# Two units' last keys and reciprocals turned together in a fused attention kernel

## The chip, the cores and the metric

The kernel runs on one core of one Trainium2 chip. The metric is the device time of one execution in microseconds (us). Engines are called as the profile calls them: PE is the matrix engine (TensorE) and PEld its weight loads, DVE the vector engine, ACT the scalar engine, POOL the general one (GpSimd), and SP the engine whose queue issues most transfers.

## The reference

Three layers follow each other on a batch of 4 sequences of 576 positions. The first is attention with 8 heads of 64 dimensions; queries and keys are rotated by position. The second is a gated two-layer product on the attention's output `x`, mixed with `x` shifted by one position. The third is a gated block with a product over positions.

```
scores = rotate(q) @ rotate(k).T / 8
attn = exp(scores - max(scores)); attn = attn / (sum(attn) + 1e-9)
x = attn @ v                                  # heads side by side: 512 columns
k = relu(mix(mu_k, x, x_prev) @ w_k) ** 2     # 512 -> 1024
x2 = sigmoid(mix(mu_r, x, x_prev) @ w_r) * (k @ w_v)
u, w = split(relu(x2 @ w_in)); w = (w - mean(w)) / sqrt(var(w) + 1e-6)
out = (u * (w_spatial @ w + b_spatial)) @ w_out
```

The change lies in the attention: where the exponentials and the reciprocal of their sum are turned (transposed) so that they can be multiplied with `v`.

## The kernel before

**Units.** Attention is cut into 72 units, 9 for each group of two head pairs, 18 for each sequence. A normal unit takes 128 query rows of one pair of heads, against all 576 keys of both heads. The fifth unit of each nine, the tail (`tail` in the code; units 4, 13, 22, ...), takes the last 64 rows of two pairs. Two normal units that follow each other share one tile `pt`, with the columns of the first at 0 to 127 and of the second at 128 to 255; `part` is 0 for the first and 1 for the second. The tail's columns stand at 256 to 319.

**The steps of a unit** (function `unit`). On PE: `scores` (L315 to L339) fills two PSUM tiles `s`, one for each head. On DVE: `top` (L342) takes the negated maximum of each head. On ACT: `expo` (L347) writes the exponentials to `p` (named `pf` in the profile) and their sums. Then `total` (L351, ACT), `norm` (L354, the reciprocal, DVE) and `spread` (L358, ACT, which writes the reciprocals 64 times side by side to `r`, named `rb`).

**Turning** is done by `turn(n)` on PE into one of two PSUM banks named `t`, and by `take(n)`, which copies the bank to `pt` and gives it free. For n = 0 and n = 1 it turns four blocks of 128 keys of head n (L378), and ACT copies 512 columns. The blocks start at key 0 for head 0 and at key 64 for head 1, so 64 keys of each are left over; they lie side by side in `p`. For n = 2 a normal unit turns these 128 keys (L380) and the spread reciprocals (L381), and DVE copies 256 columns to rows 8 and 9 of `pt`.

**Then** `values` (L402, named `v`) multiplies `pt` with `v` in 10 matrix instructions (the profile counts 20), of which the last two (four) read row 8; `gather` (L414, DVE) multiplies by row 9, the reciprocals. `values` runs after the second unit of a pair, or after the tail where the tail's columns belong to the pair too.

**The feed.** When the 18 units of a sequence are done, the second layer's first products for it (`feed`: `mk`, L498, and `mv`, L537, dots of 12 matrix instructions each) are given to PE among the units of the next sequence. The last sequence's feed has no attention beside it. Its first dot needs four chunks of mixed input, and the fourth is made from the last `gather` through a multiply (L466, ACT), an add (L470, DVE), a rounding (L476, ACT) and a difference (L479, DVE). While that feed runs, the weights of the later layers and the mixed input of the gate are loaded (`mix_steps`, L612, and the loads of L652); they wait until attention is closed.

**What sets the order.** All of this is written as steps with an engine, an estimated duration, the steps that it depends on and a rank. `Plan.order` (L62) plays the steps through: for each engine it takes, among the steps that could start soonest (on DVE and ACT within 0.3 us of that), the one of lowest rank, and it counts the room in PSUM: two `t` banks, two banks for `v` and the dots. The instructions of each engine are emitted in that order, and each engine works through its own in order. A scores step depends on both `expo` steps of the unit before, since there is only one pair of `s` tiles for each unit in flight; `expo` depends on the turns of the unit three before, whose `p` it overwrites.

After attention the remaining products (gate rows, mixing over positions, the projection) run from code written out in order (L692 to L844).

Of the kernel before, what the change touches and what calls it, by code (L numbers as in the profile page):

```python
# [7 lines left out]
F32 = mybir.dt.float32  # L8
# [8 lines left out]
B, H, S, D = 4, 8, 576, 64  # L17
# [9 lines left out]
WB, GB, WB2, GB2 = 3, 2, 3, 2  # L27
RAW, ROT, VB, PFB, PTB, XTS = 2, 4, 2, 3, 2, 6
KB, RLB, VSB = 4, 2, 1
EARLY, EVERY = 24, 2.9  # L30
# [74 lines left out]
def body(ctx: ExitStack, tc, qp, kp, vp, cs, mu_k, mu_r, w_k, w_v, w_r, w_in, w_sp, b_sp, w_out, out):  # L105
# [196 lines left out]

    units, scored, duos, freed = {}, {}, {}, {}

    def unit(m):
# [50 lines left out]
        def spread():  # L356
            st["r"] = at.tile([128, 2, D], F32, tag="rb", bufs=2, name=f"rb{m}")
            nc.scalar.copy(st["r"], st["sm"][:, 3, :].unsqueeze(2).to_broadcast([128, 2, D]))  # L358

        def turn(n, slot):  # L360
# [14 lines left out]
            elif n < 2:  # L375
                for c in range(4):
                    k = 64 * n + 128 * c
                    nc.tensor.transpose(pt[:, c, :], p[:, n, k:k + 128], ident)  # L378
            else:
                nc.tensor.transpose(pt[:, 0, :], p.rearrange("p a b -> p (a b)")[:, 512:640], ident)  # L380
                nc.tensor.transpose(pt[:, 1, :], st["r"].rearrange("p a b -> p (a b)"), ident)  # L381

        def take(n, eng):
            for u, d in enumerate(into):
                if "pt" not in d:
                    d["pt"] = at.tile([128, 10, 320], F32, tag=f"pt{d['n'] % PTB}", name=f"pt{d['n']}")
                o = d["pt"][:, 4 * n:min(4 * n + 4, 10), 256:320]
                if not tail:
                    o, x = d["pt"][:, 4 * n:min(4 * n + 4, 10), 128 * part:128 * part + 128], st["t", n]
                    x = x if n < 2 else x[:, 0:2, :]  # L390
                elif n < 2:
# [37 lines left out]
        nm = add("DVE", 0.17, norm, [t], m - 0.3)  # L429
        sp = add("ACT", 0.26, spread, [nm], m - 0.3)  # L430
        ready = [[exps[m, 0], exps[m, 1]] if tail else [exps[m, 0]], [exps[m, 1]], [sp]]
        for n in range(3):
            turned[m, n] = add("PE", (0.5, 0.5, 0.8)[n] if tail else (0.44, 0.44, 0.22)[n], lambda slot, n=n: turn(n, slot),
                               ready[n], m + 0.1 * n, take="t", kind="t")
            eng = ("ACT", "ACT", "DVE")[n]
            x = add(eng, ((0.68, 0.68, 0.55) if tail else (0.59, 0.59, 0.42))[n], lambda n=n, eng=eng: take(n, eng),
                    [turned[m, n]] + [y for d in into for y in freed.get(d["n"] - PTB, [])], m - 0.2, give=turned[m, n])
# [456 lines left out]
```

## Time and profile before

| | |
|---|---|
| median of 3 runs | 777.69 us (777.66 to 781.87) |
| profiled execution, its time | 777.82 us |
| its span | 776.0 us |
| PE busy | 740.8 us (95%) |
| DVE busy | 481.0 us (62%) |
| ACT busy | 463.6 us (60%) |
| copies out of the turned banks | ACT 160, 84.8 us; DVE 80 |
| mean granted PE clock | 0.998 |

The span runs from the first to the last instruction that the profile shows; the 1.8 us between it and the profiled execution's time lie around it. Busy shares are means over stages that are limited by different things, so the rows further down are taken by stage. A PE row can be longer than the work in it: a group of matrix instructions that waits in its middle for an operand shows the wait as part of its duration.

### The profile page before, as it was taken

The numbers are of one execution on the slowest core, as the hardware profiler recorded it, in microseconds if no ns is written. First come the engines' busy times: TensorE is split into PE (matmuls) and PEld (weight loads), VectorE is DVE, ScalarE is ACT, GpSimd is POOL, SyncE is SP. The second block draws the span as 40 slices with busy tenths as digits, with TensorE's granted clock in tenths as the row PEclk, the third lists the DMA queues.
The fourth block names the chain that finished last, engine by engine and source line by source line (L and its number), as shares of the span: only waits on it lengthen the run. The fifth ranks groups of instructions, "written<-read, shape, count | busy, mean of one in ns | idle before, by whom it ended". The sixth has DMA issues, their size and how long they took to land.

```text
span 776.0 us, 14283 instructions
## 1 busy us (share of the span) xinstructions
PE 740.8 (95%) x5696; PEld 649.9 (84%) x5696; DVE 481.0 (62%) x881; ACT 463.6 (60%) x1061; POOL 112.2 (14%) x132
## 2 busy tenths in 40 slices
PE   4788889999999999999999999999999999999997
PEld 2555569788888888888888898989989999998997
DVE  5988898888777877687856434246463342545111
ACT  3878898778777878778777644245333322533221
POOL 1432424011211211211111000002020000101000
PEclk9999999999999999999999999999999999999999
DMA  8363540542342442533232175072201212010101
GB/s 294 116 201 122 175 129 20 164 149 99 134 163 85 141 156 88 182 113 126 92 131 70 51 268 210 24 264 57 87 1 62 63 46 77 17 31 1 62 1 62
DMA packets 35268, 84.13 MB, mean 108 GB/s; under 512 B 4545, under 2 KB 10433, under 8 KB 35202
## 3 DMA queue, kind: packets, MB, share of 16 engines
q1 hardware_dynamic: 34658, 82.63, 31.6%
q8 instruction: 45, 0.74, 0.4%
q10 hardware_dynamic: 544, 0.59, 0.3%
q14 instruction: 21, 0.17, 0.1%
HBM read 60.65 MB, written 22.55 MB: 107 GB/s over the span
## 4 chain that ended last, share of the span: by engine, by line
PE 88%; DVE 4%; ACT 3%; DMA 3%; issue 0%; SPq 0%; ACTq 0%
PE mv L537 13%; PE mk L498 11%; PE v L402 11%; PE t L378 9%; PE sp L673 8%; PE r L673 7%; PE u L673 7%; PE hv L737 6%; PE o L673 6%; PE s L330 6%; PE s L338 3%; ACT pf L347 1%; DVE raw L249 1%; DMA wi<-wd 1%; PE s L327 1%; DVE sm L342 1%
## 5 line engine op out<-in xcount | busy, mean ns | idle before, releaser
L342 DVE TENSOR_REDUCE sm<-s 128x1 f32<-128x576 f32 x144 | 107.2, 751 | 36.9 <-PE s L330 30.5
L347 ACT ACTIVATE pf<-s,sm 128x576 f32<-128x576 f32 x144 | 107.0, 745 | 14.1 <-DVE sm L342 13.0
L537 PE MATMUL mv<-kh,wv 128*128 128x288 f32 x512 | 114.1, 305 | 1.2 <-ACT kh L512 1.2
L498 PE MATMUL mk<-x,wk 128*128 128x288 f32 x768 | 110.2, 298 | 0.4 <-ACT rl L505 0.4
L395 ACT COPY pt<-t 128x512 f32<-128x512 f32 (+1 forms) x160 | 84.8, 542 | 34.3 <-PE t L378 32.0
L498 PEld LDWEIGHTS mk<-x,wk 128*128 128x128 f32 x768 | 102.9, 188 | 0.7 <-ACT rl L505 0.6
L378 PE MATMUL t<-ident,pf 128*128 128x128 f32 x512 | 82.5, 284 | 14.0 <-ACT pf L347 14.0
L537 PEld LDWEIGHTS mv<-kh,wv 128*128 128x128 f32 x512 | 85.6, 191 | 5.4 <-issue 3.9
L378 PEld LDWEIGHTS t<-ident,pf 128*128 128x128 f32 x512 | 56.6, 141 | 39.9 <-issue 16.4
L402 PE MATMUL v<-pt,vt 128*64 128x256 f32 (+1 forms) x640 | 87.5, 411 | 0.0
L537 PE MATMUL mv<-kl,wv 128*128 128x288 f32 x256 | 76.5, 299 | 0.6 <-DVE kl L516 0.6
L402 PEld LDWEIGHTS v<-pt,vt 128*64 128x64 f32 x640 | 44.3, 136 | 31.7 <-issue 4.1
L673 PE MATMUL sp<-ws,vn 128*128 128x288 f32 x384 | 53.9, 295 | 0.0
L673 PE MATMUL r<-xr,wr 128*128 128x288 f32 x384 | 52.5, 296 | 1.2 <-ACT vs L543 1.2
L673 PE MATMUL o<-g,wo 128*128 128x288 f32 x384 | 52.9, 296 | 0.5 <-ACT os L796 0.5
L673 PEld LDWEIGHTS r<-xr,wr 128*128 128x128 f32 x384 | 51.7, 188 | 1.8 <-ACT vs L543 1.5
L673 PEld LDWEIGHTS sp<-ws,vn 128*128 128x128 f32 x384 | 52.4, 188 | 0.7
L673 PEld LDWEIGHTS o<-g,wo 128*128 128x128 f32 x384 | 51.7, 188 | 1.4 <-ACT os L796 1.2
L673 PE MATMUL u<-x,wi 128*128 128x288 f32 x384 | 52.0, 296 | 0.0
L673 PEld LDWEIGHTS u<-x,wi 128*128 128x128 f32 x384 | 51.6, 188 | 0.3
L537 PEld LDWEIGHTS mv<-kl,wv 128*128 128x128 f32 x256 | 48.9, 191 | 1.2 <-DVE kl L516 1.2
L249 DVE TENSOR_TENSOR raw<-raw,cst 128x1152 f32<-128x1152 f32 (+1 forms) x34 | 45.6, 1344 | 5.7 <-DMA raw<-kp 4.9
(347 smaller groups left out, 1200.3 us busy)
## 6 DMA issues: line engine op xcount, KB each, us to landing
raw<-kp SPq DMA_DIRECT2D x15, 576.0 KB, 3.8
raw<-qp SPq DMA_DIRECT2D x15, 576.0 KB, 4.3
vt<-vp SPq DMA_DIRECT2D x16, 320.0 KB, 3.8
xd<-xt SPq DMA_DIRECT2D x16, 288.5 KB, 3.2
vd<-vs SPq DMA_DIRECT2D x32, 144.0 KB, 1.8
v<-vd SPq DMA_DIRECT2D x16, 288.0 KB, 2.7
out<-os SPq DMA_DIRECT2D x15, 288.0 KB, 2.1
wi<-wd SPq DMA_DIRECT2D x8, 512.0 KB, 9.1
```

The costliest lines, as they stand in the source:

```text
L249: nc.vector.tensor_tensor(t["raw", k][:, :, z], t["raw", k][:, :, z], cst[:, :, z], op=ALU.mult)
L330: nc.tensor.matmul(ps[j][:, h, :HALF], t[a, 0][r, 128 * c:128 * c + 128], t[b, 1][r, x], **f)
L338: nc.tensor.matmul(o, q[r, 128 * c:min(128 * c + 128, S)], k[r, h * HALF:(h + 1) * HALF], start=True, stop=True)
L342: nc.vector.tensor_reduce(st["sm"][:, 0, j:j + 1], st["s"][j][:, :, :HALF], axis=AX.XY, op=ALU.max, negate=True)
L347: nc.scalar.activation(st["p"][:, j, :].rearrange("p (a b) -> p a b", a=2), st["s"][j][:, :, :HALF], AF.Exp, bias=st["sm"][:, 0, j:j + 1], ...
L378: nc.tensor.transpose(pt[:, c, :], p[:, n, k:k + 128], ident)
L395: nc.scalar.copy(o, x) if eng == "ACT" else nc.vector.tensor_copy(o, x)
L402: nc.tensor.matmul(pv[HEAD[j], z], v[:, 4 * j + c if c < 4 else 8 + j, :], pt[:, 4 * j + c if c < 4 else 8, z], start=c == 0, stop=c == 4)
L498: nc.tensor.matmul(ps[:, :HALF], wk[w][:, c, fc * 128:(fc + 1) * 128], a[:, c, :], start=k == 0, stop=k == 11)
L537: nc.tensor.matmul(xs["v", dc][:, :HALF], wv[w][:, fc, dc * 128:(dc + 1) * 128], a, start=k == 0, stop=k == 23)
L673: nc.tensor.matmul(ps[:, h, :HALF], w, a[:, h * HALF:(h + 1) * HALF], start=m == 0, stop=m == n - 1)
L737: nc.tensor.matmul(ps[:, :FS], x[a][:, d, c:c + 128], wi[w][:, d, FS:], start=k == 0, stop=k == 11)
```

## The change

The third turn is done once for two units. The first unit of a pair no longer has one; the second turns four blocks into one bank: the left-over keys of both units (positions 0 and 1 of the bank) and the spread reciprocals of both (positions 2 and 3). One DVE copy of 512 columns takes the place of two of 256. The step depends on the `spread` of both units, and the first unit's `p` and `r` have to live until then; `r` gets three tiles in place of two. The tail's third turn is as it was. The step's estimated durations change with it (0.44 for the turn, 0.68 for the copy, 0.3 for `spread`), and `THIRD` names the engine of the copy, DVE in both of its places.

```diff
--- before.py
+++ after.py
@@ -26,6 +26,7 @@
 EXACT = NP
 WB, GB, WB2, GB2 = 3, 2, 3, 2
 RAW, ROT, VB, PFB, PTB, XTS = 2, 4, 2, 3, 2, 6
+THIRD = "DVE", "DVE"
 KB, RLB, VSB = 4, 2, 1
 EARLY, EVERY = 24, 2.9
 WAIT, SWITCH, BONUS = 0.3, 0.1, 0.0
@@ -300,7 +301,7 @@
         g = 9 * (i // 2)
         return [g + 4] if i % 2 == 0 else [g + 8]
 
-    units, scored, duos, freed = {}, {}, {}, {}
+    units, scored, duos, freed, spreads = {}, {}, {}, {}, {}
 
     def unit(m):
         w = which(m)
@@ -354,7 +355,7 @@
             nc.vector.reciprocal(st["sm"][:, 3, :], st["sm"][:, 2, :])
 
         def spread():
-            st["r"] = at.tile([128, 2, D], F32, tag="rb", bufs=2, name=f"rb{m}")
+            st["r"] = at.tile([128, 2, D], F32, tag=f"rb{m % 3}", name=f"rb{m}")
             nc.scalar.copy(st["r"], st["sm"][:, 3, :].unsqueeze(2).to_broadcast([128, 2, D]))
 
         def turn(n, slot):
@@ -377,17 +378,20 @@
                     k = 64 * n + 128 * c
                     nc.tensor.transpose(pt[:, c, :], p[:, n, k:k + 128], ident)
             else:
-                nc.tensor.transpose(pt[:, 0, :], p.rearrange("p a b -> p (a b)")[:, 512:640], ident)
-                nc.tensor.transpose(pt[:, 1, :], st["r"].rearrange("p a b -> p (a b)"), ident)
+                for k in range(2):
+                    x = units[m - 1 + k]
+                    nc.tensor.transpose(pt[:, k, :], x["p"].rearrange("p a b -> p (a b)")[:, 512:640], ident)
+                    nc.tensor.transpose(pt[:, 2 + k, :], x["r"].rearrange("p a b -> p (a b)"), ident)
 
         def take(n, eng):
             for u, d in enumerate(into):
                 if "pt" not in d:
                     d["pt"] = at.tile([128, 10, 320], F32, tag=f"pt{d['n'] % PTB}", name=f"pt{d['n']}")
                 o = d["pt"][:, 4 * n:min(4 * n + 4, 10), 256:320]
-                if not tail:
-                    o, x = d["pt"][:, 4 * n:min(4 * n + 4, 10), 128 * part:128 * part + 128], st["t", n]
-                    x = x if n < 2 else x[:, 0:2, :]
+                if not tail and n == 2:
+                    o, x = d["pt"][:, 8:10, 0:256], st["t", 2].rearrange("p (k u) q -> p k (u q)", k=2)
+                elif not tail:
+                    o, x = d["pt"][:, 4 * n:4 * n + 4, 128 * part:128 * part + 128], st["t", n]
                 elif n < 2:
                     x = st["t", n].rearrange("p c (h q) -> p (c h) q", h=2)[:, 4 * u:4 * u + 4, :]
                 else:
@@ -427,13 +431,17 @@
                              m - 0.5)
         t = add("ACT", 0.2, total, [exps[m, 1]], m - 0.3)
         nm = add("DVE", 0.17, norm, [t], m - 0.3)
-        sp = add("ACT", 0.26, spread, [nm], m - 0.3)
+        sp = spreads[m] = add("ACT", 0.3, spread, [nm], m - 0.3)
         ready = [[exps[m, 0], exps[m, 1]] if tail else [exps[m, 0]], [exps[m, 1]], [sp]]
-        for n in range(3):
-            turned[m, n] = add("PE", (0.5, 0.5, 0.8)[n] if tail else (0.44, 0.44, 0.22)[n], lambda slot, n=n: turn(n, slot),
+        if not tail and part:
+            ready[2] = [spreads[m - 1], sp]
+        for n in range(3 if tail or part else 2):
+            turned[m, n] = add("PE", (0.5, 0.5, 0.8)[n] if tail else 0.44, lambda slot, n=n: turn(n, slot),
                                ready[n], m + 0.1 * n, take="t", kind="t")
-            eng = ("ACT", "ACT", "DVE")[n]
-            x = add(eng, ((0.68, 0.68, 0.55) if tail else (0.59, 0.59, 0.42))[n], lambda n=n, eng=eng: take(n, eng),
+            if n == 2 and not tail:
+                turned[m - 1, 2] = turned[m, 2]
+            eng = ("ACT", "ACT", THIRD[m >= 18] if not tail else "DVE")[n]
+            x = add(eng, ((0.68, 0.68, 0.55) if tail else (0.59, 0.59, 0.59 if eng == "ACT" else 0.68))[n], lambda n=n, eng=eng: take(n, eng),
                     [turned[m, n]] + [y for d in into for y in freed.get(d["n"] - PTB, [])], m - 0.2, give=turned[m, n])
             for d in into:
                 d["ev"].append(x)
```

The planner plays the new steps through, and the order changes at many places. Three of them are shown, all on PE. In the names, `t8_1` is turn 1 of unit 8, `s18` and `s19` are the scores of unit 9, `pf` and `rb` the exponentials and spread reciprocals, `v8` the `values` step that follows unit 8, and `mk0_0_0` the first feed dot of sequence 0.

**PE in the first 18 units, from turn 1 of unit 8.** Before:

```order
L378 MATMUL t8_1_611<-ident_95,pf8_583 128x128 x4
L380 MATMUL t8_2_616<-ident_95,pf8_583 128x128
L381 MATMUL t8_2_616<-ident_95,rb8_608 128x128
L402 MATMUL v8_622<-pt3_564,vt1_139 64x256 x10
L378 MATMUL t9_0_644<-ident_95,pf9_634 128x128 x4
L338 MATMUL s20_653<-rot2_1_437,rot2_0_466 128x288
```

With the change:

```order
L379 MATMUL t8_1_595<-ident_95,pf8_574 128x128 x4
L383 MATMUL t8_2_604<-ident_95,pf7_514 128x128
L384 MATMUL t8_2_604<-ident_95,rb7_547 128x128
L383 MATMUL t8_2_604<-ident_95,pf8_574 128x128
L384 MATMUL t8_2_604<-ident_95,rb8_601 128x128
L379 MATMUL t9_0_614<-ident_95,pf9_610 128x128 x4
L406 MATMUL v8_621<-pt3_543,vt1_139 64x256 x10
L339 MATMUL s20_650<-rot2_1_434,rot2_0_472 128x288
```

The turns of unit 7's left-over keys and reciprocals have come to unit 8's place, and `v8` now stands behind the first turn of unit 9. The same holds for `v1`, `v6` and `v15`; `v4` has gone the other way, from behind the next unit's first turn to ahead of it. `v10`, `v13` and `v17` stand as before.

**PE where the first feed dot comes in, from turn 1 of unit 18.** Before:

```order
L378 MATMUL t18_1_1166<-ident_95,pf18_1107 128x128 x4
L380 MATMUL t18_2_1175<-ident_95,pf18_1107 128x128
L381 MATMUL t18_2_1175<-ident_95,rb18_1145 128x128
L378 MATMUL t19_0_1188<-ident_95,pf19_1180 128x128 x4
L498 MATMUL mk0_0_0_1199<-x0_0_0_925,wk0_99 128x288
L498 MATMUL mk0_0_0_1199<-x1_0_0_926,wk0_99 128x288
```

With the change:

```order
L379 MATMUL t18_1_1161<-ident_95,pf18_1096 128x128 x4
L506 MATMUL mk0_0_0_1182<-x0_0_0_796,wk0_99 128x288
L506 MATMUL mk0_0_0_1182<-x1_0_0_797,wk0_99 128x288
L506 MATMUL mk0_0_0_1182<-x0_0_0_796,wk1_100 128x288
...
L506 MATMUL mk0_0_0_1182<-x0_0_0_796,wk1_100 128x288
L379 MATMUL t19_0_1204<-ident_95,pf19_1172 128x128 x4
L331 MATMUL s40_1212<-rh4_1_806,rh4_0_835 128x288
```

The dot `mk0_0_0` (12 instructions, of which three and the last one are shown) has moved from behind the first turn of unit 19 to ahead of it, right behind turn 1 of unit 18.

**PE at the end of attention, around the last `values` step, `v71`.** Before:

```order
L537 MATMUL mv2_1_3_5783<-kh2_1_1_5355,wv1_102 128x288
L402 MATMUL v71_5797<-pt31_5719,vt15_5114 64x256 x10
L537 MATMUL mv2_1_3_5783<-kh2_1_2_5458,wv0_101 128x288
...
L537 MATMUL mv2_1_3_5783<-kh2_1_3_5522,wv1_102 128x288
L498 MATMUL mk3_0_0_5849<-x0_3_0_5525,wk0_99 128x288
L498 MATMUL mk3_0_0_5849<-x1_3_0_5526,wk0_99 128x288
```

With the change:

```order
L545 MATMUL mv2_1_3_5683<-kh2_1_3_5463,wv1_102 128x288
L383 MATMUL t71_2_5739<-ident_95,pf70_5611 128x128
L384 MATMUL t71_2_5739<-ident_95,rb70_5632 128x128
L383 MATMUL t71_2_5739<-ident_95,pf71_5680 128x128
L384 MATMUL t71_2_5739<-ident_95,rb71_5710 128x128
L406 MATMUL v71_5748<-pt31_5657,vt15_5069 64x256 x10
L506 MATMUL mk3_0_0_5785<-x0_3_0_5469,wk0_99 128x288
L506 MATMUL mk3_0_0_5785<-x1_3_0_5470,wk0_99 128x288
```

Before, twelve instructions of `mv2_1_3` stand between `v71` and the last sequence's first dot `mk3_0_0`. Now they are ahead of `v71`, and `mk3_0_0` follows it directly.

## Rows read from the trace of the kernel before

**Rows 1.** Page, part 1: busy us, share of span and instructions by engine.

```profile
PE 740.8 (95%) x5696; PEld 649.9 (84%) x5696; DVE 481.0 (62%) x881; ACT 463.6 (60%) x1061; POOL 112.2 (14%) x132
```

**Rows 2.** Busy by stage: window, us busy by engine, granted clock, DMA.

```profile
0.00:20.00 20.00, 8.81 (x37) 5.09 (x38) 11.93 (x20) 8.07 (x19) 4.15 (x15) 1.00 0.84 285
20.00:108.00 88.00, 72.99 (x542) 46.21 (x540) 78.83 (x146) 73.53 (x181) 30.49 (x26) 1.00 0.45 147
108.00:448.00 340.00, 339.01 (x2904) 290.90 (x2906) 258.46 (x480) 263.16 (x658) 59.09 (x53) 1.00 0.34 117
448.00:508.00 60.00, 56.59 (x407) 54.90 (x403) 22.37 (x35) 25.63 (x54) 1.51 (x3) 0.97 0.47 165
508.00:776.00 268.00, 263.44 (x1812) 252.75 (x1810) 109.37 (x203) 93.21 (x152) 16.93 (x36) 1.00 0.18 59
```

**Rows 3.** Waits of PE, 20 to 108 us: total, times, longest.

```profile
PE t L378 <- ACT pf L347: 9.8, 9, 1.2
```

**Rows 4.** Groups by form: shapes, count, busy us, mean ns, idle before.

```profile
L395 ACT COPY pt<-t 128x512 f32<-128x512 f32 x128 | 74.5, 583 | 33.3 <-PE t L378 32.0
L395 DVE COPY pt<-t 128x256 f32<-128x256 f32 x64 | 27.1, 423 | 9.1 <-PE t L381 7.0
L395 DVE COPY pt<-t 128x128 f32<-128x128 f32 x16 | 3.8, 281 | 0.0
```

**Rows 5.** Waits of DVE up to 108 us.

```profile
DVE pt L395 <- PE t L381: 1.5, 5, 0.3
```

**Rows 6.** PE in order of time, units 8 to 10: start, us, idle before.

```profile
54.46 0.66 PE L378 MATMUL t<-ident,pf 128*128 128x128 f32 x4 [1.19 <-ACT pf L347]
...
56.48 0.66 PE L378 MATMUL t<-ident,pf 128*128 128x128 f32 x4
56.97 0.27 PE L380 MATMUL t<-ident,pf 128*128 128x128 f32 x1
57.28 2.90 PE L402 MATMUL v<-pt,vt 128*64 128x256 f32 x20
60.11 0.66 PE L378 MATMUL t<-ident,pf 128*128 128x128 f32 x4
```

**Rows 7.** ACT in order of time ahead of the turn at 54.46.

```profile
53.09 0.59 ACT L395 COPY pt<-t 128x512 f32<-128x512 f32 x1 [0.65 <-PE t L378]
53.57 0.75 ACT L347 ACTIVATE pf<-s,sm 128x576 f32<-128x576 f32 x1
```

**Rows 8.** PE in order of time: a values step with its operands ready.

```profile
114.09 2.38 PE L402 MATMUL v<-pt,vt 128*64 128x256 f32 x20
```

**Rows 9.** PE in order of time: units 1 and 5.

```profile
21.96 0.33 PE L381 MATMUL t<-ident,rb 128*128 128x128 f32 x1 [0.84 <-ACT rb L358]
...
37.78 0.65 PE L378 MATMUL t<-ident,pf 128*128 128x128 f32 x4 [0.72 <-ACT pf L347]
```

**Rows 10.** PE in order of time: unit 19 and the first dot.

```profile
108.51 0.66 PE L378 MATMUL t<-ident,pf 128*128 128x128 f32 x4 [1.19 <-ACT pf L347]
108.92 1.84 PE L498 MATMUL mk<-x,wk 128*128 128x288 f32 x12
```

**Rows 11.** DVE in order of time: the fourth chunk's differences.

```profile
108.81 0.46 DVE L479 TENSOR_TENSOR x<-mt,x 128x288 fp32r<-128x288 f32 x1
...
450.59 0.46 DVE L479 TENSOR_TENSOR x<-mt,x 128x288 fp32r<-128x288 f32 x1 [0.50 <-ACT x L476]
```

**Rows 12.** The chain of waits after attention: start, us, what.

```profile
448.48 0.44 DVE xt L414
...
451.26 0.43 SPq L652
...
458.45 8.73 DMA wi<-wd
```

**Rows 13.** PE in order of time after that load.

```profile
469.42 0.40 PE L537 MATMUL mv<-kh,wv 128*128 128x288 f32 x1 [1.24 <-ACT kh L512]
```

**Rows 14.** Busy by stage, with the granted clock, around that load.

```profile
460.00:480.00 20.00, 17.80 (x117) 16.72 (x116) 12.55 (x20) 11.77 (x24) 0.00 (x0) 0.91 0.82 297
```

## The prediction

> **What bounds the kernel now.** I read the page first, then busy time by stage, then the waits of PE by stage, then the order of time in the places that the change touches. The page [rows 1] shows PE busy for 95% of the span, DVE and ACT for about 60%. The stages [rows 2] say where the other 5% lies. Up to 20 us the operands come in. From 20 to 108 us, about the first 18 units, PE is busy for 73.0 of 88 us, DVE for 78.8 and ACT for 73.5: three engines hand work to each other, none is full. From 108 to 448 us the feed fills PE: 339.0 of 340 us. From 448 to 508 us 3.4 us are missing, and the rest does not know of this change. So the change can win or lose time in two ways: through what PE waits for in the first 108 us and around 448 us, or through the work that PE has to do anywhere else.
>
> In the first 108 us the wait that comes back is that of a unit's first turn for its exponentials, 9.8 us in nine places [rows 3]. One such place shows the mechanism [rows 6, 7]. Turn 1 of the unit before ends at 53.07; ACT copies that bank from 53.09, starts the exponentials at 53.57, and PE can start the next turn at 54.46. So from the end of a turn 1 to the next turn 0 some 1.39 us pass, and the third turn, where it stands between them, only fills 0.24 us of them.
>
> **The change, part by part.**
>
> *PE's work.* The transposes stay: four where there were two and two. In the row of four at 56.48, with the next at 56.97, each takes 0.12 us [rows 6]. PE's sum is unchanged: 0. In the 340 us where PE is full nothing else counts, as long as DVE (258 of 340 us) and ACT (263) keep up [rows 2], so I take 0 there; the planner's new order there is unknown in its waits, and I allow 1.5 us either way, about what PE lacks today.
>
> *DVE's work.* 64 copies of 423 ns go, 32 of 512 columns come. The trace has no DVE copy of that size: from 128 to 256 columns the mean rises from 281 to 423 ns [rows 4], and twice that slope more gives 0.71 us. Below it stands ACT's copy of 512 columns, 0.58 us, above it two old copies, 0.85 us. By the middle value DVE saves 64 x 0.423 - 32 x 0.707 = 4.5 us, of which eight of the 32 pairs, 1.1 us, lie ahead of 108 us. DVE sets no chain there for long, so I count 0; the rival below counts it.
>
> *The odd units of the first 18, three places.* At `v6`, `v8` and `v15` the planner now puts the next unit's first turn ahead of the `values` step. Before, turn 1 starts at 56.48 and the next turn 0 at 60.11: 3.63 us hold turn 1, the third turn and `values` [rows 6]. This `values` step is 2.90 us long where one with its operands ready takes 2.38 [rows 8]: 0.52 us in it are a wait for the copies. Now turn 1 (0.66 us by its row) is followed by the 1.4 us that the exponentials need; the four transposes fill 0.48 of them and PE stands for 0.9. Turn 0 follows, and then `values` without its wait, 2.31 us from start to start (2.83 less 0.52). That is 0.66 + 1.39 + 2.31 = 4.36 against 3.63 us, a loss of 0.73, in three places 2.2 us. The wait in `values` that went was smaller than the one that comes. Nothing is lost at the even units: the gap behind their turn 1 is the same 1.39 us, with or without the two transposes in it.
>
> *The first pair.* `v1` moves in the same way, but there the third turn waited 0.84 us for the spread reciprocals of unit 1 [rows 9], behind two long DVE instructions. Without the copy of unit 0 ahead of these, DVE reaches them about 0.5 us sooner. Net loss 0.2 us (between 0 and 0.73).
>
> *The first tail.* `v4` moves ahead of unit 5's first turn, which waits 0.72 us today [rows 9]; `values` fills that. Against it stand the two more transposes (0.24) and the longer copy (0.28), which lie between the two maxima of the tail, so that its second maximum comes 0.5 us later. Gain 0.2 us (between a loss of 0.5 and a gain of 0.7).
>
> *Where the feed begins.* `mk0_0_0` moves into the gap ahead of unit 19's first turn. There PE stands for 1.19 us today, and the dot starts only after that turn [rows 10]. The most that can be won is the gap, 1.4 us. The dot's last three instructions need the fourth input chunk, whose difference ends at 109.27 today [rows 11], 0.4 us after the dot starts but well ahead of its end. Pulled forward by 1.5 us, the dot waits for that chunk until about 109.3 and ends near 109.5; turn 0 then ends near 110.1 where before the dot ended near 110.7. I take 0.8 us won (between 0 and 1.4).
>
> *The end of attention.* `mk3_0_0` loses its cover. The gather starts at 448.48 behind the last `values` step [rows 12], and the chunk's difference ends at 451.05 [rows 11]. Today twelve instructions, 1.6 us, stand in between; now the dot reaches its fourth chunk 1.2 us after `values` and waits 2.6 - 1.2 = 1.4 us. But today's chain does not run through PE here. It runs through the loads of the later weights, issued from 451.26, to one that lands at 467.2 [rows 12]; behind that DVE and ACT are late and PE stands at 469.42 for 1.24 us [rows 13]. In the window around it the granted clock is 0.91 [rows 14], between the two levels of 1.2 and 2.4 GHz: for some 3.6 of 20 us the lower one was granted, which costs 1.8 us of work. The loads were held by a store of the last `mv` dot; that dot now ends ahead of `values`, and the loads can go 0.3 us sooner after the same amount of PE work. So the 1.4 us should come out of the later wait: 0.3 us won, and I add 0.5 for a part of the clock's loss. Term: -0.8 us, between -1.8 (the clock's whole loss saved) and +1.4 (the wait comes on top).
>
> **The sum.** +2.2 + 0.2 - 0.2 - 0.8 - 0.8 = +0.6 us. Against the profiled execution's own 777.82 us (span 776.0) this gives 778.4; the median of the three runs is 777.69, so the two agree to 0.02%. Forecast: no change, **778.4 us**.
>
> **The rivals.**
>
> *The lost covers are paid (slower).* One mechanism: a feed dot that stands directly behind the `values` step which makes its fourth chunk. It has two places, `mk0_0_0` and `mk3_0_0`. If the chunk is late in the first, its gain falls to 0; if PE still waits more than about 1.2 us behind the load at the end, the 1.4 us are paid on top. From there on: 0.6 + 0.8 + 0.8 + 1.4 = +3.6 us, 781.4. For it: the chain of gather, multiply, add, rounding and difference is in the rows with its 2.6 us. Against it: PE is not the late one at the end. Chance 0.25.
>
> *DVE is the bound of the first stage (faster).* It is the busiest there, 78.8 of 88 us. Then the 2.2 us of the three places vanish beside work that DVE has to do anyway, and DVE wins its 1.1 us and the waits for the third turn, 1.5 us up to 108 us [rows 5]. With the other terms: 0.2 - 0.2 - 0.8 - 0.8 - 2.6 = -4.2 us, 773.6. Against it: at 54.46 PE waits for exponentials that stood behind an ACT copy, not behind DVE [rows 6, 7]. Chance 0.17.
>
> *The larger copy is late wherever it is needed (slower by over 1%).* The copy starts 0.24 us later and is 0.28 us longer. If each of the 32 `values` steps waited for it, that is 32 x 0.52 = 16.6 us, 794.4. It decides if row 8 of `pt` is needed within 0.7 us of the third turn's end. Against it: only the last two products of a `values` step read that row, over 1.8 us after its start by the 2.38 us of [rows 8]. The Trainium skill has the rule behind this rival (Perfetto Trace Analysis, Optimizing Scalar/DVE Operations): grouping helps an engine that is saturated, and where it is not but makes others wait, instructions are better broken up. By that rule this change goes the wrong way. The trace agrees with its condition (DVE not full) but not with its consequence, since what PE waits for is ACT's exponentials. Chance 0.04.
>
> **How the numbers follow.** The forecast case has 0.52 (its own range 775.8 to 780.8, from the bounds of the terms), the slower rival 0.25, the faster 0.17, the late copy 0.04; 0.02 is left for an order in the full stage that makes PE wait much. About 1% (7.8 us) is what a measurement of this kernel tells from no change. None of the first three cases reaches that, so: faster 0.02, within 1% 0.92, slower 0.06. The range holds the forecast and reaches to both neighbours: 773.6 to 781.6.
>
> **What would show it.** DVE shows 32 copies of 128x512 near 0.71 us and none of 256; PE as many transposes as before. At `v8` the next turn 0 stands ahead of `values` with a wait of about 0.9 us, and `values` is 2.4 us long. PE's idle from 20 to 108 us for exponentials grows by about 2 us. The first dot stands ahead of unit 19's first turn without a long wait. At the end of attention PE waits about 1.4 us in `mk3_0_0` and less behind the load; if both waits stand there, the slower rival is right. If the time falls by 3 us or more while the waits at `v6`, `v8` and `v15` are there, the reading of the first stage is wrong: those units then had slack that I did not see. If PE drops below 338 of 340 us in the full stage, the planner's order costs there what I took as nothing.

## The result

The changed kernel takes **788.38 us** in the median (784.69 to 789.44, 4 runs), the kernel before 778.5 in the same comparison: 1.011 times as long, with an interval of 1.0065 to 1.0156. Forecast were 778.4 us, in a range up to 781.6. The change is slower, by more than any case that I had given a real chance.

The profiled execution of the changed kernel took 788.16 us, its span is 786.2. Below is the busy time from its page (us, share, instructions), which answers to [rows 1].

```profile
PE 746.0 (95%) x5696; PEld 653.5 (83%) x5696; DVE 474.8 (60%) x849; ACT 461.4 (59%) x1061; POOL 111.2 (14%) x132
```

DVE works 6.2 us less (4.5 forecast), and PE, with the same instructions, is busy for 5.2 us more. The stages say why. The columns are those of [rows 2]: window, its length, busy time of PE, PEld, DVE, ACT and POOL, granted clock, share of DMA, GB/s.

```profile
20.00:108.00 88.00, 69.32 (x483) 44.28 (x480) 70.84 (x124) 64.54 (x162) 28.96 (x25) 0.92 0.41 135
108.00:448.00 340.00, 338.44 (x2885) 288.48 (x2885) 257.47 (x464) 265.85 (x668) 60.35 (x54) 1.00 0.37 119
448.00:508.00 60.00, 56.66 (x424) 53.61 (x423) 24.69 (x39) 27.65 (x59) 1.50 (x3) 1.00 0.46 160
508.00:776.00 268.00, 266.26 (x1833) 255.60 (x1832) 109.69 (x203) 93.58 (x154) 16.35 (x36) 1.00 0.17 57
```

The granted clock of PE in the first stage was 1.00 and is 0.92. That is the number to read first: 8% of 88 us, some 7.0 us of PE's work at its full rate (what is lost is less, since PE also stood for part of that time), and no engine is busier for it. It is not spread evenly, as the same view of PE alone shows (busy time of PE, clock, DMA).

```profile
20.00:40.00 20.00, 15.77 (x131) 1.00 0.38 122
40.00:60.00 20.00, 15.35 (x96) 0.91 0.48 160
60.00:80.00 20.00, 16.21 (x121) 1.00 0.42 143
80.00:100.00 20.00, 16.32 (x104) 0.74 0.44 143
...
84.00:88.00 4.00, 3.85 (x33) 0.50 0.46 156
88.00:92.00 4.00, 3.73 (x14) 0.50 0.79 239
```

There are two stretches, one behind 45 and one from 83 to 93 us, in which PE runs at the lower of its two levels (0.50 is 1.2 of 2.4 GHz). What does PE do before them? The waits of PE from 20 to 108 us (total, times, longest) answer to [rows 3].

```profile
PE t L379 <- ACT pf L348: 13.6, 11, 2.3
PE t L368 <- ACT pf L348: 3.7, 4, 1.0
```

The wait of a first turn for its exponentials grew from 9.8 to 13.6 us. None of the waits is longer than 2.3 us. The first stretch, from PE in order of time (start, us, idle before), begins with that longest one, at unit 6's first turn:

```profile
42.95 0.66 PE L379 MATMUL t<-ident,pf 128*128 128x128 f32 x4
45.88 1.12 PE L379 MATMUL t<-ident,pf 128*128 128x128 f32 x4 [2.27 <-ACT pf L348]
46.93 2.29 PE L339 MATMUL s<-rot,rot 64*128 64x288 f32 x8
...
82.06 0.46 PE L368 MATMUL t<-ident,pf 64*128 64x64 f32 x4 [0.98 <-ACT pf L348]
83.39 0.58 PE L368 MATMUL t<-ident,pf 64*128 64x64 f32 x3 [0.87 <-ACT pf L348]
...
83.87 2.23 PE L339 MATMUL s<-rot,rot 64*128 64x288 f32 x7
...
89.31 4.97 PE L406 MATMUL v<-pt,vt 128*64 128x320 f32 x20
94.21 1.24 PE L339 MATMUL s<-rot,rot 64*128 64x288 f32 x8
```

A turn takes 1.12 us where it takes 0.66, a scores step 2.29 where it takes 1.24 to 1.50, and the wide `values` step behind the second tail 4.97 where the one at 51.80 takes 2.91. A group that is nearly twice as long, with nothing written behind it, is how the lower level looks in the rows.

The 2.27 us have their own story. `v4` now stands ahead of unit 5's first turn, so its `gather` came into another place of DVE's queue, behind a long rotation product. DVE in order of time:

```profile
41.22 2.43 DVE L250 TENSOR_TENSOR raw<-raw,cst 128x1152 f32<-128x1152 f32 x1
43.58 0.48 DVE L418 TENSOR_TENSOR xt<-v,pt 128x320 f32<-128x320 f32 x1
```

and ACT, whose next instruction, a multiply for the feed, needs that `gather`, with the copy and the exponentials behind it:

```profile
44.09 0.54 ACT L474 ACTIVATE mt<-xt,mix 128x288 f32<-128x288 f32 x1 [1.61 <-DVE xt L418]
44.53 0.56 ACT L399 COPY pt<-t 128x512 f32<-128x512 f32 x1
44.99 0.74 ACT L348 ACTIVATE pf<-s,sm 128x576 f32<-128x576 f32 x1
```

In the kernel before, the same turn waits 1.19 us:

```profile
44.45 0.66 PE L378 MATMUL t<-ident,pf 128*128 128x128 f32 x4 [1.19 <-ACT pf L347]
```

When the scores of a unit start tells where the time goes (us, from both traces; at all these units PE has done the same work in both):

| scores of unit | 6 | 8 | 10 | 14 | 15 | 17 | 21 | 30 | 48 | 66 |
|---|---|---|---|---|---|---|---|---|---|---|
| before | 41.21 | 51.22 | 60.70 | 79.27 | 86.11 | 96.13 | 116.99 | 176.60 | 291.36 | 406.00 |
| after | 41.78 | 54.65 | 64.73 | 83.66 | 94.21 | 104.83 | 124.99 | 183.71 | 300.58 | 416.20 |
| later by | 0.6 | 3.4 | 4.0 | 4.4 | 8.1 | 8.7 | 8.0 | 7.1 | 9.2 | 10.2 |

Two steps, 2.9 us from unit 6 to 8 and 3.7 from unit 14 to 15, hold the two stretches. The rest of the first stage comes to 1.4 us. In it lies a third place: PE of the changed kernel comes to its full rate later. The same turn and scores step, in the kernel before and with the change:

```profile
17.95 0.66 PE L378 MATMUL t<-ident,pf 128*128 128x128 f32 x4 [1.19 <-ACT pf L347]
18.54 1.89 PE L338 MATMUL s<-rot,rot 64*128 64x288 f32 x8
...
18.02 1.11 PE L379 MATMUL t<-ident,pf 128*128 128x128 f32 x4 [1.41 <-ACT pf L348]
19.07 2.48 PE L339 MATMUL s<-rot,rot 64*128 64x288 f32 x8
```

The granted clock of the window from 0 to 20 us reads 1.00 in both kernels, so this place shows in the lengths of the rows alone. Against the same steps at the full rate, the rows of the three places are longer by about 1.5 us (up to 22 us), 1.4 (from 46 us) and 4.4 (from 83 us). This estimate, 7.3 us together, leaves less than 1 us of the 8.0 for the waits themselves. Some 2 us more are lost in the full stage, of which I had taken none.

### The profile page after: what moved, and what is told of

Its sections match the earlier page's. It is cut to its first block, busy times and chain, and to the rows that moved or that the text cites. A ratio compares the mean times of both kernels' runs of the same rounds, so it can differ in the third digit from the quotient of the medians.

```text
span 786.2 us, 14259 instructions
## 1 busy us (share of the span) xinstructions
PE 746.0 (95%) x5696; PEld 653.5 (83%) x5696; DVE 474.8 (60%) x849; ACT 461.4 (59%) x1061; POOL 111.2 (14%) x132
## 4 chain that ended last, share of the span: by engine, by line
PE 88%; ACT 5%; DMA 4%; DVE 3%; SPq 1%; issue 0%; ACTq 0%
PE mv L545 11%; PE mk L506 11%; PE v L406 10%; PE t L379 9%; PE sp L681 8%; PE r L681 7%; PE u L681 7%; PE hv L745 6%; PE o L681 6%; PE s L331 6%; PE s L339 4%; ACT pf L348 2%; DMA I-5925_5926<-xd 1%; PE s L328 1%; ACT pt L399 1%; PE t L368 1%
## 5 line engine op out<-in xcount | busy, mean ns | idle before, releaser
L343 DVE TENSOR_REDUCE sm<-s 128x1 f32<-128x576 f32 x144 | 104.6, 751 | 40.7 <-PE s L331 28.6
L506 PE MATMUL mk<-x,wk 128*128 128x288 f32 x768 | 113.3, 300 | 2.4 <-ACT vs L551 0.9
L545 PE MATMUL mv<-kh,wv 128*128 128x288 f32 x512 | 108.5, 299 | 1.2 <-ACT kh L520 1.2
L379 PE MATMUL t<-ident,pf 128*128 128x128 f32 x512 | 84.4, 289 | 18.2 <-ACT pf L348 18.2
L545 PEld LDWEIGHTS mv<-kh,wv 128*128 128x128 f32 x512 | 83.7, 188 | 2.3 <-ACT kh L520 1.4
```

The costliest lines, as they stand in the source:

```text
L343: nc.vector.tensor_reduce(st["sm"][:, 0, j:j + 1], st["s"][j][:, :, :HALF], axis=AX.XY, op=ALU.max, negate=True)
L506: nc.tensor.matmul(ps[:, :HALF], wk[w][:, c, fc * 128:(fc + 1) * 128], a[:, c, :], start=k == 0, stop=k == 11)
L545: nc.tensor.matmul(xs["v", dc][:, :HALF], wv[w][:, fc, dc * 128:(dc + 1) * 128], a, start=k == 0, stop=k == 23)
```

## The experiments

Theory A: the waits in the first stage cost themselves, and as much again through a lower clock. Rivals: B, the pairing itself delays `values`; C, the planner's other order in the full stage. All times are medians; the ratio is that to the kernel before on the same chip, with its 95% interval. The clock is that of PE from 20 to 108 us, and "unit 21" how much later than in the kernel before its scores start, both in the profiled execution.

| run | us | before | ratio | clock | unit 21 |
|---|---|---|---|---|---|
| the change | 788.38 | 778.5 | 1.0110 (1.0065 to 1.0156) | 0.92 | +8.0 |
| e1_values_first | 787.64 | 778.66 | 1.0109 (1.0078 to 1.0140) | 0.94 | +9.8 |
| e2_before_turn_first | 788.31 | 778.66 | 1.0111 (1.0087 to 1.0135) | 0.90 | +11.0 |
| e3_fill | 782.37 | 778.66 | 1.0047 (1.0031 to 1.0063) | 0.98 | +5.4 |
| e4_late_pairs | 782.01 | 778.66 | 1.0036 (1.0021 to 1.0051) | 1.00 | -1.5 |
| e3b_fill_before | 781.35 | 778.55 | 1.0037 (1.0022 to 1.0052) | 1.00 | +2.4 |
| e4b_early_pairs | 785.27 | 778.55 | 1.0084 (1.0062 to 1.0106) | 0.92 | +9.1 |
| e5_copy_only | 781.17 | 778.55 | 1.0043 (1.0023 to 1.0062) | 0.94 | +6.2 |
| e6_early_fill | 782.26 | 778.52 | 1.0055 (1.0041 to 1.0068) | 1.00 | +3.4 |
| e7_early_fill2 | 783.06 | 778.52 | 1.0059 (1.0047 to 1.0071) | 0.96 | +5.1 |
| e8_old_order | 787.33 | 778.5 | 1.0128 (1.0085 to 1.0172) | 0.93 | +8.3 |
| e9_one_place | 782.46 | 778.5 | 1.0034 (1.0009 to 1.0058) | 0.96 | +6.1 |
| e10_order_fill | 784.33 | 778.5 | 1.0075 (1.0049 to 1.0101) | 1.00 | +5.2 |

(With late pairs one feed dot of 1.58 us stands behind unit 21's scores that stood ahead of it; without that it is +0.1. The profiled execution is one run and not the median: it took 784.51 us in e3, 789.1 in e4b, 781.66 in e6. And the last column holds -0.5 to +1.0 us that stand ahead of the first scores already, most in e5 and e9.)

### Is it the order of `values` and the next turn?

**e1_values_first**, after the planner has made its order:

```diff
     def emit(self):
-        for s in self.order():
+        steps = self.order()
+        for x, y in self.moves:
+            if steps.index(x) < steps.index(y):
+                steps.remove(x)
+                steps.insert(steps.index(y) + 1, x)
+        for s in steps:
...
+            if n == 0 and m - 1 in (1, 6, 8, 15):
+                plan.moves.append((turned[m, 0], stepv[m - 1]))
```

> The changed kernel with one thing moved on PE alone: at v1, v6, v8 and v15 the next unit's turn 0 stands behind the values step again, as it did before the change. DVE, ACT and the queues keep the changed kernel's order. Theory A (waits of PE in the first stage cost themselves and, by a lowered granted clock, as much again): the three waits of 0.97 us ahead of turn 0 go, the half-rate stretch behind 80 us shrinks or goes, the one at 44 to 52 us, which begins at unit 6's turn 0, stays: 780 to 784 us against 788.4. Theory B (the pairing itself delays values, through the late third turn and the larger copy): the values steps wait about as long as turn 0 did, 786 us or more. Theory C (the planner's other order in the full stage costs the time): no change, 788.

Measured 787.64 us: what theory A said of this run fails. The waits ahead of the turns 0 at `v6`, `v8` and `v15` are gone and the one ahead of unit 6's first turn has stayed, as expected, but others have come. PE of this kernel in order of time:

```profile
48.05 1.11 PE L387 MATMUL t<-ident,pf 128*128 128x128 f32 x4 [2.28 <-ACT pf L356]
...
62.85 0.33 PE L392 MATMUL t<-ident,rb 128*128 128x128 f32 x1 [0.67 <-ACT rb L367]
...
107.92 0.66 PE L387 MATMUL t<-ident,pf 128*128 128x128 f32 x4 [2.80 <-ACT pf L356]
...
109.83 1.11 PE L387 MATMUL t<-ident,pf 128*128 128x128 f32 x4
110.74 0.42 PE L391 MATMUL t<-ident,pf 128*128 128x128 f32 x1
```

At `v8` the joint third turn now waits 0.67 us for the reciprocals, and from scores to scores that place takes 6.32 us, where the changed kernel has 6.26: nothing is won there, as theory B said. The lower level now also starts behind 2.80 us ahead of unit 17's first turn. Which place pays has changed, the sum has not. So the three places of my prediction are not the cause by themselves.

**e2_before_turn_first** is the counterpart, in the kernel before:

```diff
+            if n == 0 and m - 1 in (1, 6, 8, 15):
+                plan.moves.append((stepv[m - 1], turned[m, 0]))
```

> The kernel before, every third turn by itself, with the one move on PE: at v1, v6, v8 and v15 the values step stands behind the next unit's turn 0, as in the changed kernel. Theory A: the waits ahead of these turns come without any pairing, some 0.7 us net in each of four places, and the clock falls behind one or two of them: 781 to 785 us against 778.5, with a granted clock below 1.00 between 20 and 108 us. Theory B: no pairing, no loss beyond the waits themselves, 779 to 781 us with the clock at 1.00 there.

Measured 788.31 us, more than theory A's upper end, with no pairing at all. Four moved steps on PE, with DVE and ACT in their old order, cost as much as the whole change. The windows and PE in order of time at `v8`:

```profile
60.00:80.00 20.00, 16.76 (x91) 0.74 0.44 142
20.00:108.00 88.00, 69.45 (x474) 0.90 0.41 135
```

```profile
65.21 1.11 PE L393 MATMUL t<-ident,pf 128*128 128x128 f32 x4 [2.05 <-ACT pf L362]
66.26 4.54 PE L417 MATMUL v<-pt,vt 128*64 128x256 f32 x20
```

Here the moved turn waits 2.05 us, not the 0.97 of the changed kernel, and `values` takes 4.54 us.

**e8_old_order** puts PE's whole old order back into the first stage of the changed kernel; e1 with one move more:

```diff
+            if n == 0 and m == 5:
+                plan.moves.append((stepv[4], turned[5, 0]))
```

> The changed kernel with PE's whole old order in the first stage: values ahead of the next turn 0 at v1, v6, v8 and v15, and v4 behind unit 5's turn 0. What stays of the change there is that two units' third turns stand together behind the odd unit's turn 1, and the joint copy. If the fall of the clock comes from these two (the gap behind every even unit's turn 1 has lost its two transposes): 785 to 789 us, clock 0.91 to 0.96 from 20 to 108 us. If it comes from v4, which moved unit 6's long wait: 781 to 784 us.

Measured 787.33 us, clock 0.93: the first branch. The clock falls even in PE's old order, so `v4` alone is not it. What stays of the change is the two turns taken together, the joint copy, and also the planner's new order of DVE and ACT, which this run keeps; it does not tell these apart.

**e9_one_place**: e2 with `(8,)` in place of `(1, 6, 8, 15)`.

> The kernel before with one move on PE: v8 stands behind unit 9's turn 0. If one more wait of about 0.9 us is enough to bring the clock down: 780 to 785 us, a stretch at the lower level within some 20 us behind unit 9's turn 0, at about 57 us. If it takes several of them: the wait alone, 0 to 0.7 us, 778 to 780 us, clock 1.00.

Measured 782.46 us, but its runs spread from 780.52 to 786.3. At the place itself the first branch holds, though behind a wait of 2.05 us and not of 0.9; PE in order of time:

```profile
62.09 0.66 PE L393 MATMUL t<-ident,pf 128*128 128x128 f32 x4 [2.05 <-ACT pf L362]
62.67 4.07 PE L417 MATMUL v<-pt,vt 128*64 128x256 f32 x20
```

From unit 8 to unit 10 this costs 3.3 us. But 2.7 of the 6.1 us at unit 21 are lost ahead of unit 6, where nothing was moved: 0.9 ahead of the first scores, 0.5 up to unit 3, and the rest in a stretch at the lower level that the profiled execution of the kernel before does not have. What one wait costs in the mean is therefore not settled by this run.

One thing is common to the traces. In each of the nine kernels whose clock falls between 20 and 108 us, one of the falls lies within 1 us of the start of unit 5's or unit 14's scores. There a tail is turned and PE waits twice in a row: 0.98 and 0.87 us in the changed kernel at unit 14, 1.19 and 0.47 us in the kernel before. Why the clock falls there of all places is not shown.

### Is it the clock, or only the waits?

**e3_fill**, the changed kernel with work put into the waits:

```diff
         def turn(n, slot):
...
             p = st["p"]
+            if n == 0 and 0 < m < 18:
+                for c in range(4):
+                    nc.tensor.transpose(pt[:, c, :], ident, ident)
```

> The changed kernel, and ahead of every turn 0 of units 1 to 17 PE turns the identity four times into the bank that this turn then writes over, 17 x 4 transposes of 0.12 us, 8.3 us of added work of which up to 0.5 us per unit lies in the wait for the exponentials. Order and data are those of the changed kernel. Theory A: the waits are shorter to the clock, the half-rate stretches go (5 to 6 us back), and where a turn 0 did not wait the fill costs up to 0.5 us: 782 to 787 us with the granted clock at 1.00 from 20 to 108 us. Theory B or C: the clock is no cause but a mark of the same delay; the added work can only cost, 789 to 793 us.

Measured 782.37 us. Eight us of work were added for PE, and the kernel became 6.0 us faster (4.9 by the two ratios). Its windows (columns as above):

```profile
20.00:40.00 20.00, 17.51 (x139) 12.06 (x140) 14.33 (x30) 15.14 (x41) 8.08 (x7) 1.00 0.35 118
40.00:60.00 20.00, 17.30 (x123) 11.25 (x120) 17.09 (x27) 14.98 (x39) 6.67 (x6) 1.00 0.49 167
...
80.00:100.00 20.00, 17.05 (x130) 12.10 (x132) 18.36 (x36) 15.16 (x41) 6.69 (x4) 0.91 0.50 158
...
20.00:108.00 88.00, 76.62 (x573) 52.14 (x572) 73.76 (x132) 67.97 (x171) 30.89 (x26) 0.98 0.41 136
```

One stretch at the lower level is left, at 84 us. Order, data and the chain through ACT and DVE are those of the changed kernel; only PE stands less, 7.7 us for exponentials where it was 13.6. Added work can't shorten that chain, so what came back is PE's rate. This is what separates the clock from the waits. It holds for all runs and not for the profiled one alone: the mean granted clock over the span was 0.987 to 0.993 in the changed kernel's four runs and 0.995 to 1.000 in the twelve with the fill.

**e3b_fill_before** is the control, the same lines in the kernel before.

> The kernel before with the same fill as in the run before: four turns of the identity ahead of every turn 0 of units 1 to 17. Theory A (in the changed kernel the fill won because it held the clock): the kernel before has its clock at 1.00 in this stage already, so here the fill wins nothing; it lies in the waits for the exponentials for the most part: 778 to 782 us. Rival (the fill wins by something else, such as an earlier full rate at the start, or the timing of the copies): 773 to 776 us.

Measured 781.35 us: where the clock stood at 1.00 already, the same fill costs 2.8 us. The clock with it:

```profile
20.00:108.00 88.00, 80.57 (x590) 1.00 0.43 138
```

With the fill in both kernels the change costs 782.37 - 781.35 = 1.0 us, which the two intervals don't tell from nothing.

**e10_order_fill**: the four moves of e2 and the fill together.

> The kernel before with the four moves (788.3 us by themselves) and the fill of four turns of the identity ahead of every turn 0 of units 1 to 17. If what the moves cost is for the most part the clock, the fill brings back what it brings back in the changed kernel, about 6 us: 781 to 784 us, clock 0.98 or more from 20 to 108 us. If the moves cost through late values and copies, the fill wins nothing: 787 us or more.

Measured 784.33 us, 4.0 us faster than e2 without the fill (the two intervals just overlap), at the edge of what theory A allowed. The clock:

```profile
20.00:108.00 88.00, 77.38 (x569) 1.00 0.43 136
```

Against e3b the four moves cost 3.0 us by themselves, where the 0.73 us that the prediction gave to such a place would make 2.9. That these agree is chance: against e3b's trace, `v8` costs 1.7 us here and each of the other three about 0.3. Without the fill the moves cost 9.7. The other 6.7 us came back with the fill, and the clock with them: over the span it was 0.987 to 0.991 in e2's runs and 0.995 to 0.999 in these.

### Which part of the change?

**e4_late_pairs** and **e4b_early_pairs** do it in one stage each; the second with `m < 18`:

```diff
+    paired = lambda m: m >= 18
...
-        if not tail and part:
+        if not tail and part and paired(m):
             ready[2] = [spreads[m - 1], sp]
-        for n in range(3 if tail or part else 2):
+        for n in range(3 if tail or part or not paired(m) else 2):
```

> Third turns are taken together from unit 18 on, and one by one in units 0 to 17 as in the kernel before. Theory A: the first 108 us are those of the kernel before (clock 1.00), and what the changed kernel lost behind 124 us, about 2 us, remains at most: 777 to 781 us. Theory C (the order in the full stage): 784 us or more.

> Third turns are taken together in units 0 to 17 alone, and one by one from unit 18 on. Theory A with the reading that the changed kernel's loss has two parts, 3.4 us behind unit 18 (the run with late pairs) and the rest, 6 to 7 us, in the first stage: 784 to 787 us, with a granted clock of 0.90 to 0.95 from 20 to 108 us. Rival (the two parts are not independent, the first stage alone brings the loss): 788 us or more.

Measured 782.01 us (a little above theory A's end) and 785.27: 3.4 and 6.7 us, together 10.1 of the change's 9.9. The greater part is the first stage, but theory C has a part in it too.

That part shows in the changed kernel. In the kernel before, 14 of the scores steps from unit 20 on stand directly behind a feed dot, in the changed one none does; nearly all stand behind a first turn. A scores step needs the tiles that the unit before still reads, and in three places they are late. PE of the changed kernel in order of time:

```profile
233.44 0.40 PE L331 MATMUL s<-rh,rh 64*128 64x288 f32 x1
234.07 0.53 PE L331 MATMUL s<-rh,rh 64*128 64x288 f32 x3 [0.23 <-ACT pf L348]
...
263.57 0.52 PE L331 MATMUL s<-rh,rh 64*128 64x288 f32 x3 [0.42 <-ACT pf L348]
...
350.93 0.53 PE L331 MATMUL s<-rh,rh 64*128 64x288 f32 x3 [0.24 <-ACT pf L348]
```

The idle time in brackets is only part of it: these steps take 1.6 to 1.8 us from their start to the next turn (1.00 without a wait), and behind each of them the shift against the kernel before is 0.9 to 1.2 us larger, once the feed dots that stand elsewhere are counted. A wait after a step's first instruction hides in its length.

**e5_copy_only** takes half of the change: the joint copy, with all transposes where they were.

```diff
+    joint = lambda m: m < 18 and m % 9 != 4
...
+            if n == 2 and joint(m):
+                if not part:
+                    st["t2"] = ps_m.tile([128, 512], F32, tag=f"m{1 - last[0]}", name=f"t{m}_2")
+                else:
+                    st["t2"] = units[m - 1]["t2"]
+                pt = st["t", n] = st["t2"].rearrange("p (c q) -> p c q", c=4)[:, 2 * part:2 * part + 2]
...
+            if n == 2 and joint(m) and not part:
+                return
```

> Half of the change, in units 0 to 17 alone: one copy for two units, but every unit's two transposes stay where the kernel before has them. The first unit's pair of results waits in a bank of the ring of values for the second's. PE and ACT have the order of the kernel before, instruction for instruction; on DVE the eight copies of even units are gone and eight larger ones stand in the odd units. From unit 18 on it is the kernel before. Theory A (the moved transposes and the planner's order lower the clock, not the joint copy): 776 to 780 us, clock 1.00. Theory B (the joint copy delays values): a values step would wait up to 0.3 us longer in eight places, 780 to 782 us without, or 784 and more with a fall of the clock.

Measured 781.17 us, with a clock of 0.94 in the profiled execution: theory B's time without a fall of the clock, though the clock fell. `values` waits for the larger copy, as the waits of PE from 20 to 108 us show:

```profile
PE t L387 <- ACT pf L349: 9.5, 9, 1.2
PE v L416 <- DVE pt L408: 3.9, 5, 0.8
```

These 3.9 us are not all new. At `v6`, `v8`, `v10` and `v15` PE stands 0.78 to 0.81 us ahead of `values`, but in the kernel before about 0.5 us are hidden inside each of these steps (2.90 us at `v8`, where one with its operands ready takes 2.38). So some 0.3 us are new at each, as I had expected. Fewer and larger copies cost here even with the order unchanged, and the clock was lower with them. That these waits brought it down is not shown: its two falls, at 35 and 83 us, stand at the tails, where PE's second wait is 0.66 us instead of 0.40 and 0.47.

**e6_early_fill** and **e7_early_fill2** are e4b with the fill of e3, with four and with two turns of the identity.

> Third turns together in units 0 to 17 alone (785.3 us by itself), with the fill of four turns of the identity ahead of every turn 0 of units 1 to 17. If the clock is what the first stage loses, the fill wins the 6 us here too, with the stage behind unit 18 as in the kernel before: 778 to 781 us, unit 20's scores within 1.5 us of the kernel before. If the fill won 6 us in the whole change by something in the later stage, it wins little here: 783 us or more.

> The same with two turns of the identity instead of four, 0.24 us in each wait. If what counts is how much PE stands still, half the fill gives back a part: 779 to 783 us, with the clock of the first stage between 0.95 and 1.00. If the clock is kept by any work in the wait, however little, 777 to 779 us, a little better than with four.

Measured 782.26 us, 3.0 less than e4b (their intervals just overlap), with the first stage at 1.00. It is 1.3 more than the expectation's upper end, and unit 20's scores are 3.0 us late where 1.5 were expected: the fill's own cost, 2.4 us there by e3b, was left out of it. With half the fill it is 783.06, at a clock of 0.96: the second run's first branch.

None of the runs beats the kernel before. How much one wait costs in the mean stays open. So does why the late pairs cost 3.1 to 3.4 us without the fill (e4, and the change against e4b) and only 0.1 with it (e3 against e6), but the traces narrow this. From unit 21 to unit 71 e3 falls back by 2.2 us against the kernel before, as the changed kernel does, while e6 gains 0.2: the loss in the full stage is there with the fill too. What hides it in the medians is probably the clock, which over the span was 0.9985 in the median of e3's runs and 0.994 in e6's; where e6's runs lose it, its one trace, of a run with 0.998, does not show.

## Why the prediction was wrong

**The step that failed** is the one that costs PE's waits in the first stage: "in three places 2.2 us", and with it the list of rivals. It counted a wait of PE at its own length. As lengths the terms were good: at `v8` and `v15`, where nothing else happens, the stretch from scores to scores grew by 0.6 us each (0.73 forecast), PE stands 0.97 us ahead of the next turn 0 (0.9), and `values` takes 2.38 us at `v8`. With the fill in both kernels the change costs 1.0 us (0.6 forecast), which proves little, since the fill itself stands in the waits that the terms price. Up to unit 21 the terms make +1.4 us (2.2 + 0.2 - 0.2 - 0.8), and 8.0 were measured. What was missing is a second price: in the stage with these waits PE ran at its lower level for longer, which made its rows some 7 us longer, and e3, e3b and e10 show that this is the greater part of the loss and that it comes back when PE is kept at work. Which of the waits bring the clock down is not shown: e2, e5 and e8 have it fall with other waits than those of the change.

The clue stood in the prediction itself. [rows 14] show 0.91 in the only 20 us of the kernel before in which the clock fell, with a wait of 1.24 us in them [rows 13]. I used this as a gain at the end of attention, and did not ask what the same would cost in a stage to which the change adds waits of 0.9 us and takes the third turn out of the gap behind every even unit. The Trainium skill names the effect (TensorE: Matmul & The Clock Gate, HAM oscillation): a kernel whose PE waits again and again for operands begins each piece of work at the lower rate. Its example waits for transfers, and longer. The trace agrees in kind but not in length: here PE waited for exponentials, and for at most 2.27 us at a time.

**The first tail** was forecast to gain 0.2 us (at most 0.7); up to unit 6 it won 0.7, but the moved `gather` made unit 6's first turn wait 2.27 us where the kernel before waits 1.19 there. That queue, DVE's and then ACT's, I had not followed. **The first pair** lost more than 0.7: unit 3's scores start 1.25 us late. PE reaches its full rate later there, and the 1.5 us by which the rows are longer are all of it, so that the term itself was near its 0.2.

**The full stage** was taken as 0, 1.5 us either way. Three late scores steps cost 0.9 to 1.2 us each, and where a third turn had waited in the kernel before, some 0.7 come back. The sign that I had named, PE below 338 us of 340, did not show it (338.44): the waits hide inside the steps.

**Right in size:** where the feed begins 0.7 us were won (0.8), and `mk0_0_0` waits 0.41 us in its middle.

**The end of attention** was forecast to gain. `mk3_0_0` waits for its fourth chunk, as forecast, but the wait behind the load stands almost whole, 1.19 us where it was 1.24. Both waits are there, the sign that I had named for the slower rival; PE of the changed kernel there:

```profile
460.13 1.45 PE L506 MATMUL mk<-x,wk 128*128 128x288 f32 x9
462.37 11.87 PE L506 MATMUL mk<-x,wk 128*128 128x288 f32 x85 [0.79 <-ACT x L484]
...
479.84 0.40 PE L545 MATMUL mv<-kh,wv 128*128 128x288 f32 x1 [1.19 <-ACT kh L520]
```

The clock there is 1.00 now, the waits together are longer (4.6 us from unit 71's scores to the first product behind the feed, against 3.4), and the two cancel: 0.0 where I had -0.8. The overlap that I had counted on is not there, and only the clock made up for it. The joint copy of 512 columns takes 690 ns (707 forecast).

```profile
L399 DVE COPY pt<-t 128x512 f32<-128x512 f32 x32 | 22.1, 690 | 18.2 <-PE t L384 18.2
```

**The rivals.** Of the two lost covers, the one at `mk0_0_0` was not paid; the one at `mk3_0_0` was, and the clock gave it back. DVE was no bound. The larger copy came late after all in e5, by 0.3 to 0.7 us more than before in six of the first eight places; in the change itself its wait does not show, since PE already stands for exponentials. The rule of the Trainium skill that I had set beside it (Perfetto Trace Analysis, Optimizing Scalar/DVE Operations) was right about the direction: DVE was not full, and in e5 larger pieces of work made PE wait longer.

**The range.** Added up, the bounds of the terms give 774.6 to 784.1 us, and not the 775.8 to 780.8 of the forecast case; the measured time lies above both. And 1% was too much for what a measurement tells from no change: e3b's interval, 1.0022 to 1.0052, does not reach 1.

## What to carry to other kernels

Where PE is neither full nor idle, a wait on it can have two prices, its own length and what the clock takes afterwards; look at the granted clock by short windows, before the change for what is at stake and after it for what was lost. Before taking small work out of a gap, or grouping it, ask what then fills the gap: here grouping saved 6.2 us of DVE's work and cost 9.9 us of the kernel's time. To tell the two prices apart, put work that changes nothing into the waits, in both kernels.

## What was not expected of the hardware

Adding 8.3 us of PE work (68 transposes of 0.12 us) made the changed kernel 6.0 us faster. And the kernel before does not have its clock for certain: in the last comparison its 19 runs took 776.31 to 784.17 us at a mean granted clock of 0.999 to 0.988 over the span, the six of 782 us and more all at 0.988.
